# Streaming halves of weight blocks through six 2 KB places, keeping the other halves in pairs, and copying o1 in two parts

## The chip, the cores and the metric

The kernel runs as one program on one core of a Trainium2 chip. The metric is device time in microseconds (us) of one execution. Three runs of the kernel before took 2072.62, 2074.7 and 2076.44 us; the time that counts is their median, 2074.7 us.

## The reference, cut to what matters

Two independent heads share the output, and their results stand side by side in it. Head B is a long convolution over 2048 positions (by Fourier transforms) and does not change here. Head A is a recurrence over 64 segments of 32 rows, with a memory of 8 rows that each segment hands to the next:

```python
for s in range(n_seg):                                   # 64 segments
    xs = x[:, s * seg_len:(s + 1) * seg_len, :].copy()   # 32 rows
    h = jnp.concatenate([mem, xs], axis=1)               # 8 + 32 rows of 1024
    q = jnp.einsum('btd,dhe->bhte', h, Wq)               # 32 heads of 128
    k = jnp.einsum('btd,dhe->bhte', h, Wk)
    v = jnp.einsum('btd,dhe->bhte', h, Wv)
    scores = jnp.einsum('bhqe,bhke->bhqk', q, k) * scale
    scores = jnp.where(mask[None, None], scores, -1000000000.0)
    p = _softmax(scores, axis=-1)
    o = jnp.einsum('bhqk,bhke->bhqe', p, v)
    o = jnp.einsum('bhte,hed->btd', o, Wo)
    mem = o[:, :M, :].copy()                             # the next segment needs these 8 rows
    outs.append(o[:, M:, :])
```

So each segment multiplies by all of Wq, Wk, Wv and Wo, four bf16 matrices of 1024 x 4096 (8 MB each), and can begin only when the one before it has ended. The four matrices do not fit on the chip together with the rest.

## The kernel before, in words

**Stages.** Part B of the program (head B) fills the first 700 us. Beside it, work of head A that does not depend on the recurrence is done ahead: of every segment, 24 rows form, with the 8 memory rows, the 32 rows of the loop (the tile `hT`), and the keys, queries and values of the last 8 rows are computed before the loop and stored to DRAM (`PKd`, `VXd`). Then part A's loop over 64 segments runs (lines 357 to 583), and behind it one large product makes the output rows of those last 8 rows of all segments (lines 585 to 616).

**Weight blocks.** The weights are cut into 64 blocks of 128 rows by 2048 columns in bf16: 512 KB, or 4 KB in each of the 128 partitions. A block of k, q or v is named by matrix, column half t and row block kc; a block of o by u from 0 to 15, and holds two heads of 1024 columns each. A segment uses each block once, in one order: k of t = 0, q of t = 0, k and q of t = 1, v of t = 0, v of t = 1, then o 0 to 15.

**Where a block lies.** 49 blocks stay in SBUF (`RESIDENT`, loaded by `load_resident`, most of them during part B into places that part B has given up, the last 11 by `unit` in the first segment, where they are first used). Three blocks lie wholly or by half in PSUM (`KEPT`) and are copied out in each segment by VectorE (`fetch`, line 292). The other 12 (`STREAM`, `STREAM_O`) are loaded again in every segment: k 1 + 2, q 1 + 1, v 2 + 2, o 3. Before the loop they are copied to DRAM tiles of their own (`WD`, by `streamed_copies`, DRAM to DRAM during part B). In the loop `stage` (line 297) loads one whole block by one DMA of SyncE into the next of `SLOTS` = 4 places in turn (the tiles `wst`), so 16 KB of a partition serve as places. A load is issued as soon as the block that had the place, four loads earlier, has been used by TensorE. SyncE issues all of them in program order, and in the steady loop it issues nothing else; the loads of `PKd` and `VXd` and the two stores of a segment go out from ScalarE's DMA queue.

**The products.** In `quads` (line 365) a block of k, q or v takes 4 matmuls with 512 columns, one for each group of 32 columns of the array, side by side; in `oproj` (line 474) a block of o takes 8 with 256 columns. The weight columns are the moving operand. Four such matmuls together advance TensorE by about 0.21 us.

**The end of a segment.** `pv_x` makes the values of the second half of the heads in PSUM; `evac_o` (line 460) copies them to SBUF on ScalarE as `o1`, 128 x 512 in one instruction, while TensorE runs `oproj` for o 5, 6, 7 with `o0`. Then `oproj` for o 8 to 15 reads `o1`: an even u reads heads 0 and 1 of each group of four, an odd u heads 2 and 3. The output row block is copied (line 567), turned (line 573), and its memory rows enter `hT` (line 575) for the next segment. SBUF work tiles of the loop lie in one tile, `arena`.

In the traces an L365 or L474 matmul that reads `wst` reads a streamed block; one that reads `W`, `W_k`, `W_v`, `W_o`, `MF`, `Wlow` reads a resident one.

Of the kernel before, what the change touches and what calls it, by code (L numbers as in the profile page):

```python
# [10 lines left out]
BF16 = mybir.dt.bfloat16  # L11
# [10 lines left out]

STREAM = {("k", 0): (2,), ("q", 0): (2,), ("k", 1): (1, 5), ("q", 1): (4,), ("v", 0): (2, 7), ("v", 1): (4, 7)}
STREAM_O = (4, 8, 13)

BANK = {("k", 0): "b0", ("q", 0): "b1", ("k", 1): "b2", ("q", 1): "b0", ("v", 0): "b3", ("v", 1): "b2"}
KEPT = {("k", 0, 7): (("K7a", 0, 512), ("K7b", 512, 512), ("K7c", 1024, 512), ("K7d", 1536, 384), (None, 1920, 128)),
        ("q", 0, 7): (("Q7a", 1024, 512), ("Q7b", 1536, 512)),  # L30
        ("o", 15): (("Oa", 1024, 512), ("Ob", 1536, 384), (None, 1920, 128))}
HALF = (("q", 0, 7), ("o", 15))
SLOTS = 4

ARENA = 5984
AT = {"K7a": 3072, "K7b": 1024, "K7c": 2048, "K7d": 4192, "ob": 4960, "pk": 0, "vx": 3392, "Q7a": 2048, "Q7b": 3072,
# [18 lines left out]
    return src  # L55


def streamed_keys():
    return [key for key in [(m, t, kc) for (m, t), kcs in STREAM.items() for kc in kcs] + [("o", u) for u in STREAM_O]]


def streamed_copies(ctx, tc, src):
    nc = tc.nc
    dram = ctx.enter_context(tc.tile_pool(name="a_wd", bufs=1, space=bass.MemoryType.DRAM))
    out, copies = {}, []
    for key in streamed_keys():
        t_ = dram.tile([128, 2048], BF16, name="WD_%s" % "_".join(str(i) for i in key))
        copies.append(lambda t_=t_, key=key: nc.sync.dma_start(
            out=t_[:].rearrange("e (h d) -> e h d", h=2) if key[0] == "o" else t_[:], in_=src(key)))
        out[key] = t_  # L70
    return out, copies


class Ahead:
# [136 lines left out]
    return hT  # L211


RESIDENT = [(m, t, kc) for t in range(2) for m in "kq" for kc in range(8)] + [("v", t, kc) for t in range(2) for kc in range(8)] + [("o", u) for u in range(16)]
RESIDENT = [key for key in RESIDENT if key not in streamed_keys() and key not in KEPT]


class Keys(list):
    pass


EARLY = (3, 5)
LATE = 5


def load_resident(tc, pool, src, key, W_res, eng=None, t_=None):
    if t_ is None:
        t_ = pool.tile([128, 2048], BF16, name="W_%s" % "_".join(str(i) for i in key))
    (eng or tc.nc.sync).dma_start(out=t_[:].rearrange("e (h d) -> e h d", h=2) if key[0] == "o" else t_[:], in_=src(key))
    W_res[key] = t_  # L230


def part_a(ctx, tc, x, src, WD, HE, seg_len, out_a, ahead, W_res, rest, places, first):
    nc = tc.nc
    S, Dm = x.shape
    M = 8
    SL = seg_len
# [21 lines left out]
    between = {}  # L259

    def unit(key):
        if key in rest:

            rest.remove(key)
            load_resident(tc, wres, src, key, W_res, None, places.pop(0)() if places else None)
        if key in W_res:
            return W_res[key]
        if key in KEPT:
            return ahead_of.pop(key) + halves.get(key, [])
        between.pop(key, lambda: None)()  # L270
        if key in first:
            return first.pop(key)
        return stage(key, WD[key][:])

    ctx_l = ctx_w.enter_context(ExitStack())
    pers = ctx_l.enter_context(tc.tile_pool(name="a_pers", bufs=1))
# [14 lines left out]
    def words(out, in_):  # L291
        nc.vector.tensor_scalar(out=out.bitcast(I32), in0=in_.bitcast(I32), scalar1=0, scalar2=None, op0=ALU.bitwise_or)  # L292

    def stage(key, in_):
        t_ = wst.tile([128, 2048], BF16, name="wst", tag="w%d" % (loads[0] % SLOTS))
        loads[0] += 1
        nc.sync.dma_start(out=t_[:].rearrange("e (h d) -> e h d", h=2) if len(in_.shape) == 3 else t_[:], in_=in_)
        return t_

    def load_kept(key):  # L300
        t_ = first.pop(key) if key in first else stage(key, src(key))
        kept[key] = {}
        for n in (1,) if key in HALF else (0, 1):
            kept[key][n] = ps_k.tile([128, 512], F32, name="keep", tag="keep%d" % sum(len(b) for b in kept.values()))
            words(kept[key][n][:], t_[:, 1024 * n:1024 * n + 1024])
        if key in HALF:
            t_ = ahead.low["half"] if key[0] == "q" else wres.tile([128, 1024], BF16, name="Whalf")
            nc.sync.dma_start(out=t_[:], in_=src(key)[:, 0, :] if key[0] == "o" else src(key)[:, 0:1024])
            halves[key] = [(0, 1024, t_)]

    def fetch(key):
# [45 lines left out]
    for s in range(NS):  # L357
# [97 lines left out]
            pv(p[:], t, V, pb.rearrange("p a b c -> p a (b c)"), lbs)  # L455
            return p

        def evac_o(p, name):
            o = at(name, 4, 4, SL)
            nc.scalar.copy(out=o, in_=p[:].rearrange("p a (g q) -> p a g q", g=4))  # L460
            return o

        def pv_l(pl, t, V, L):
# [47 lines left out]
        nc.scalar.copy(out=QT1, in_=p1[:, 1])  # L511
        if s + 1 == NS:

            spare = [W_res[m, t, kc] for m, t in (("k", 0), ("q", 0), ("k", 1), ("q", 1), ("v", 0)) for kc in range(KC) if (m, t, kc) in W_res]
# [67 lines left out]
        if s + 1 < NS:  # L582
            stores(s, ob)

    order = sorted(range(16), key=lambda u: ("o", u) not in W_res)
    wo = {}
    for u in order:
        if ("o", u) in W_res:
            wo[u] = W_res["o", u]
        else:  # L590
            wo[u] = spare.pop(0)
            if ("o", u) in WD:
                nc.sync.dma_start(out=wo[u][:], in_=WD["o", u][:])
            else:
                nc.sync.dma_start(out=wo[u][:].rearrange("e (h d) -> e h d", h=2), in_=src(("o", u)))
    stores(NS - 1, ob)
    for j in range(2, 8):
        nc.sync.dma_start(out=raw[j][:], in_=OLd[j])
# [4 lines left out]
    for b in range(4):  # L603
        pe = [ps_k.tile([128, 512], F32, name="pe", tag="keep%d" % (2 * (b % 2) + n)) for n in range(2)]
        for u in order:
            for hh in range(2):
                h = 2 * u + hh
                hi = 16 * (h // 16) + 4 * (h % 4) + (h % 16) // 4
                for n in range(2):
                    nc.tensor.matmul(pe[n][:], lhsT=left[2 * b + hi // 16][:, 128 * (hi % 16):128 * (hi % 16) + 128],  # L610
                                     rhs=wo[u][:, 1024 * hh + 512 * n:1024 * hh + 512 * n + 512], start=(u == order[0] and hh == 0),
                                     stop=(u == order[-1] and hh == 1))
# [782 lines left out]
def kernel(  # L1395
# [33 lines left out]

    def residents(stay, early):  # L1430
        def put(t_):
            load_resident(tc, None, src, rest.pop(0), W_res, None, t_)
# [36 lines left out]

    low = low_blocks(ctx, tc)  # L1470
    ahead.low = low.pop()
    copies += [lambda t_=t_: load_resident(tc, None, src, rest.pop(0), W_res, None, t_) for t_ in low]

    def first_state(m0, xt):
        nc = tc.nc
# [49 lines left out]
```

## Time and profile before

| | us |
|---|---|
| three runs | 2072.62, 2074.7, 2076.44 (median 2074.7) |
| the profiled execution, its own time | 2080.33 |
| its span, first to last instruction | 2078.6 |
| part A's first segment (line 365's first matmul to the first transpose of line 573) | 705.45 to 753.47 |
| the next 62 segments, from transpose to transpose | 753.47 to 1996.36 |
| last segment and closing product | 1996.36 to 2078.6 |
| TensorE busy over the span | 1877.4 (90%) |
| weight loads of TensorE busy | 1188.3 (57%) |
| VectorE, ScalarE, GpSimd busy | 1415.5, 1047.8, 380.1 |
| mean granted TensorE clock | 0.975 |

The page gives busy shares for each engine and slices of the span in tenths; the queues' table gives the packets, bytes and the share of the core's 16 DMA engines that they took. "Idle before" a group of instructions is the idle time of its engine just before them, with what ended it. Matmuls overlap in the records, so a matmul's duration (382 ns) is longer than the time by which it moves TensorE on.

### The profile page before, as it was taken

What the parts mean: (1) busy time and instruction counts of PE and PEld (TensorE: products, weight loads), DVE (VectorE), ACT (ScalarE), POOL (GpSimd) and SP (SyncE); (2) the same over time, 40 slices, a digit from 0 to 9 for tenths busy, and PEclk for the clock granted to TensorE, in tenths of its full rate; (3) what the DMA queues carried; (4) which work ended last, traced back from release to release, by engine and by line L of the source; (5) the groups of instructions that cost most, each with busy time, mean ns of one, the idle gap of its engine ahead of it and who ended that gap; (6) DMA issues with size and microseconds to landing.
All of it is one profiled execution on the core that took longest, in us unless ns stands there. A gap on an engine that the chain in (4) does not pass through costs nothing. (4 is left out here: it accounts for less than half of the span.)

```text
span 2078.6 us, 78528 instructions
## 1 busy us (share of the span) xinstructions
PE 1877.4 (90%) x33734; PEld 1188.3 (57%) x33734; DVE 1415.5 (68%) x3352; ACT 1047.8 (50%) x1917; POOL 380.1 (18%) x748
## 2 busy tenths in 40 slices
PE   2799999977999779999999999999999999999999
PEld 1365666756888545555555555555555555555554
DVE  8689999989899346566666666656666666666650
ACT  5899999961333334444444444444444444444430
POOL 2133343452000011111111111111111111111120
PEclk8799999989999889999999999999999999999999
DMA  7697985665646999999999999999999999999991
GB/s 192 168 254 214 260 233 172 163 201 191 213 137 189 317 348 331 330 334 337 330 339 341 335 341 332 340 323 335 345 331 341 336 338 336 344 340 335 328 351 47
DMA packets 351187, 590.78 MB, mean 284 GB/s; under 512 B 108537, under 2 KB 228377, under 8 KB 348789
## 3 DMA queue, kind: packets, MB, share of 16 engines
q1 hardware_dynamic: 297016, 528.00, 75.4%
q10 hardware_dynamic: 44812, 28.26, 4.4%
q0 software_dynamic: 9008, 29.49, 4.3%
q8 instruction: 264, 4.33, 0.8%
q14 instruction: 87, 0.70, 0.1%
HBM read 530.86 MB, written 65.26 MB: 287 GB/s over the span
## 5 line engine op out<-in xcount | busy, mean ns | idle before, releaser
L365 PEld LDWEIGHTS <-a_hT 128*32 128x32 bf16 x12352 | 340.3, 96 | 294.1 <-issue 45.5
L371 ACT CAST arena<-acc 128x512 bf16<-128x512 f32 x384 | 225.1, 586 | 392.2 <-PE acc L365 333.6
L365 PE MATMUL acc<-W,a_hT 128*32 128x512 bf16 x4608 | 361.0, 382 | 0.6 <-issue 0.6
L474 PEld LDWEIGHTS <-arena 128*32 128x32 bf16 x8256 | 209.6, 96 | 110.2 <-ACT arena L460 54.7
L365 PE MATMUL acc<-wst,a_hT 128*32 128x512 bf16 x2304 | 231.9, 382 | 15.7 <-DMA wst<-WD_v 7.9
L292 DVE TENSOR_SCALAR arena<-keep 128x256 int32<-128x256 int32 (+1 forms) x512 | 176.2, 395 | 38.2 <-PE acc L365 35.1
L379 POOL COPY arena<-arena 128x128 bf16<-128x128 bf16 x128 | 37.6, 294 | 872.7 <-DMA arena<-PKd 311.4
L365 PE MATMUL acc<-MF,a_hT 128*32 128x512 bf16 x2048 | 172.5, 384 | 0.2 <-issue 0.2
L474 PE MATMUL pp<-W_o,arena 128*32 128x256 bf16 x4096 | 149.3, 275 | 5.4 <-DMA W_o<-in_A_Wo_dram 5.2
L167 PE MATMUL pro<-xTl,wsl 128*128 128x512 bf16 x512 | 123.0, 393 | 7.0 <-ACT xTl L111 4.9
L414 DVE TENSOR_REDUCE a_mx<-sc 128x4 f32<-128x160 f32 (+1 forms) x192 | 73.0, 380 | 82.4 <-ACT sc L410 82.4
L406 DVE TENSOR_REDUCE a_mx<-sc 128x4 f32<-128x160 f32 (+1 forms) x192 | 71.9, 374 | 79.5 <-PE sc L394 78.2
L1059 PEld LDWEIGHTS <-MF 128*128 128x128 bf16 x1024 | 103.1, 101 | 29.8 <-issue 8.6
L410 ACT ACTIVATE sc<-sc 128x160 f32<-128x160 f32 (+1 forms) x192 | 63.9, 333 | 108.0 <-DVE sc L407 85.1
L489 DVE COPY arena<-tr 128x512 bf16<-128x512 bf16 x64 | 27.2, 425 | 130.1 <-PE tr L376 130.1
L437 POOL TENSOR_TENSOR arena<-arena,a_BD 128x128 bf16<-128x128 bf16 x128 | 70.7, 552 | 227.7 <-DVE arena L424 204.6
L1059 PE MATMUL hps<-KT,MF 128*128 128x256 bf16 x720 | 94.7, 284 | 14.3 <-DVE x L1228 11.2
L567 ACT CAST arena<-pp 128x128 bf16<-128x128 f32 x128 | 27.7, 269 | 156.9 <-PE pp L474 156.9
L1286 PE MATMUL yp<-Bt,MI 128*128 128x256 bf16 x680 | 104.6, 274 | 0.8 <-ACT yb L1302 0.8
L1097 ACT ACTIVATE E<-pa 128x648 bf16<-128x648 f32 x128 | 91.4, 714 | 18.8 <-PE pa L1089 13.9
L460 ACT CAST arena<-pv 128x512 bf16<-128x512 f32 x128 | 75.3, 588 | 50.3 <-PE pp L444 39.7
L474 PE MATMUL pp<-wst,arena 128*32 128x256 bf16 x1536 | 77.2, 277 | 23.5 <-DMA wst<-WD_o 14.1
(313 smaller groups left out, 3976.0 us busy)
## 6 DMA issues: line engine op xcount, KB each, us to landing
wst<-WD_v SPq DMA_DIRECT2D x256, 512.0 KB
wst<-WD_k SPq DMA_DIRECT2D x192, 512.0 KB
wst<-WD_o SPq DMA_DIRECT2D x192, 512.0 KB
wst<-WD_q SPq DMA_DIRECT2D x128, 512.0 KB
Ud<-ux POOLq DMA_DIRECT2D x16, 1024.0 KB, 5.1
uq<-Ud SPq DMA_DIRECT2D x32, 512.0 KB
wsl<-in_A_Wk_dram SPq DMA_DIRECT2D x16, 512.0 KB
wsl<-in_A_Wv_dram SPq DMA_DIRECT2D x16, 512.0 KB
```

What stands on the lines that cost most here:

```text
L167: nc.tensor.matmul(a[:], lhsT=w[:, kc, 128 * j:128 * j + 128], rhs=xTl[:, kc, :, :].rearrange("p s k -> p (s k)"), start=(kc == 0), stop=( ...
L292: nc.vector.tensor_scalar(out=out.bitcast(I32), in0=in_.bitcast(I32), scalar1=0, scalar2=None, op0=ALU.bitwise_or)
L365: nc.tensor.matmul(a[32 * g:32 * g + 32, o_:o_ + rhs.shape[1]], lhsT=hT[:, kc, :], rhs=rhs, start=(kc == 0), stop=(kc == KC - 1), tile_pos ...
L371: nc.scalar.copy(out=q, in_=a[:])
L406: nc.vector.tensor_reduce(out=m_, in_=x, axis=AX.X, op=ALU.max)
L414: nc.vector.tensor_reduce(out=m_, in_=x, axis=AX.X, op=ALU.add)
L437: nc.gpsimd.tensor_tensor(out=L[:, 0].rearrange("p (a b) k -> p a b k", a=4), in0=bc(lt[:, :, 0:XL].unsqueeze(2), [128, 4, 4, XL]), in1=bc ...
L460: nc.scalar.copy(out=o, in_=p[:].rearrange("p a (g q) -> p a g q", g=4))
L474: nc.tensor.matmul(po[32 * qt:32 * qt + 32, o_:o_ + rhs.shape[1]], lhsT=oT[:, h % 4, (h % 16) // 4, :], rhs=rhs, start=False, stop=(h == 3 ...
L1059: pe.matmul(s_[r][half][:, cs, :], lhsT=MF[:, kc, 4 * rr + mc, cs, :], rhs=rhs, start=(i == 0 and mc == 0), stop=(i == 1 and mc == 3), ski ...
L1097: sc.activation(out=T["E", r, e // 4][:, lo:lo + 8 * NE].rearrange("p (i c) -> p i c", i=2), in_=T.pop(("p", r, e))[:, :, 0:4 * NE], func= ...
L1286: pe.matmul(yp[:, b, :], lhsT=m_[:, b, cs, kc, :], rhs=Bt[:, kc, j, half, c_, :], start=(kc == 0 and cs == 0 and half == 0), stop=(kc == 3 ...
```

## The change

`STREAM` now lists halves of blocks: 22 halves of 22 different blocks, each 128 x 1024 (256 KB, 2 KB in a partition). `SLOTS` is 6, and a place holds 2 KB, so 12 KB of a partition serve as places. The other halves of these 22 blocks stay in SBUF, two to one tile of 4 KB (`resident_items`), so there are 50 resident tiles, one more than before; one more is loaded early (`EARLY`). The DRAM tiles are 128 x 1024, and `streamed_copies` returns 11 functions that each issue two copies. `unit` returns both halves of a block as a list, which `columns` already accepts. `load_kept` stages halves, and of two of the kept blocks only the half that goes to PSUM. `o1` is copied in two instructions of 128 x 256, heads 0 and 1 of each group first, and `oproj` takes o 8, 10, 12, 14 before 9, 11, 13, 15. Behind the loop the closing product fills halves instead of whole blocks.

```diff
-STREAM = {("k", 0): (2,), ("q", 0): (2,), ("k", 1): (1, 5), ("q", 1): (4,), ("v", 0): (2, 7), ("v", 1): (4, 7)}
-STREAM_O = (4, 8, 13)
+STREAM = ((("k", 0, 2), 0), (("k", 0, 5), 1), (("q", 0, 2), 0), (("q", 0, 6), 1), (("k", 1, 2), 1), (("k", 1, 3), 0),
+          (("k", 1, 6), 0), (("q", 1, 1), 1), (("q", 1, 5), 1), (("v", 0, 1), 1), (("v", 0, 3), 1), (("v", 0, 7), 1),
+          (("v", 1, 2), 1), (("v", 1, 3), 1), (("v", 1, 4), 0), (("v", 1, 5), 1), (("o", 0), 0), (("o", 4), 1),
+          (("o", 6), 1), (("o", 10), 0), (("o", 11), 0), (("o", 13), 1))
...
-SLOTS = 4
+SLOTS = 6
...
+def part(src, key, h):
+    return src(key)[:, h, :] if key[0] == "o" else src(key)[:, 1024 * h:1024 * h + 1024]
...
+    for key, h in STREAM:
+        out[key, h] = dram.tile([128, 1024], BF16, name="WD_%s" % "_".join(str(i) for i in (*key, h)))
+
+    def copy(some):
+        for key, h in some:
+            nc.sync.dma_start(out=out[key, h][:], in_=part(src, key, h))
+    return out, [lambda i=i: copy(STREAM[i:i + 2]) for i in range(0, len(STREAM), 2)]
...
-EARLY = (3, 5)
+EARLY = (3, 6)
...
+        out = []
+        for h in range(2):
+            half = key, h
+            for item in [item for item in rest if half in item]:
+                rest.remove(item)
+                load_resident(tc, wres, src, item, W_res, places.pop(0)() if places and len(item) == 2 else None)
+            if half in W_res:
+                out.append((1024 * h, 1024, W_res[half]))
+            else:
+                out.append((1024 * h, 1024, first.pop(half) if half in first else stage(WD[half][:])))
+        return out
...
-    def stage(key, in_):
-        t_ = wst.tile([128, 2048], BF16, name="wst", tag="w%d" % (loads[0] % SLOTS))
+    def stage(in_):
+        t_ = wst.tile([128, 1024], BF16, name="wst", tag="w%d" % (loads[0] % SLOTS))
         loads[0] += 1
-        nc.sync.dma_start(out=t_[:].rearrange("e (h d) -> e h d", h=2) if len(in_.shape) == 3 else t_[:], in_=in_)
+        nc.sync.dma_start(out=t_[:], in_=in_)
         return t_
 
     def load_kept(key):
-        t_ = first.pop(key) if key in first else stage(key, src(key))
         kept[key] = {}
         for n in (1,) if key in HALF else (0, 1):
+            t_ = first.pop((key, n)) if (key, n) in first else stage(part(src, key, n))
...
-        def evac_o(p, name):
-            o = at(name, 4, 4, SL)
-            nc.scalar.copy(out=o, in_=p[:].rearrange("p a (g q) -> p a g q", g=4))
+        def evac_o(p, name, parts=1):
+            o, n = at(name, 4, 4, SL), 4 // parts
+            for i in range(0, 4, n):
+                nc.scalar.copy(out=o[:, i:i + n], in_=p[:, i:i + n, :].rearrange("p a (g q) -> p a g q", g=4))
             return o
...
-        o1 = evac_o(pv1, "o1")
+        o1 = evac_o(pv1, "o1", 2)
...
-        oproj(pp[:, 1, :], range(8, 16), o1)
+        oproj(pp[:, 1, :], (8, 10, 12, 14, 9, 11, 13, 15), o1)
...
-        for i, key in enumerate([("k", 0, 7)] + streamed_keys()[0:SLOTS - 1]):
-            first[key] = t_ = ahead.wst.tile([128, 2048], BF16, name="wst", tag="w%d" % i)
-            tc.nc.sync.dma_start(out=t_[:], in_=WD[key][:] if key in WD else src(key))
-            yield
+        for i, half in enumerate([(("k", 0, 7), 0), (("k", 0, 7), 1)] + list(STREAM[0:SLOTS - 2])):
+            first[half] = t_ = ahead.wst.tile([128, 1024], BF16, name="wst", tag="w%d" % i)
+            tc.nc.sync.dma_start(out=t_[:], in_=WD[half][:] if half in WD else part(src, *half))
+            if i % 2:
+                yield
```

More of the change, by code (lines that the diff above doesn't have):

```diff
@@ L55, in weight_blocks @@
     return src
-def streamed_keys():
-    return [key for key in [(m, t, kc) for (m, t), kcs in STREAM.items() for kc in kcs] + [("o", u) for u in STREAM_O]]
+def part(src, key, h):
+    return src(key)[:, h, :] if key[0] == "o" else src(key)[:, 1024 * h:1024 * h + 1024]
 def streamed_copies(ctx, tc, src):
@@ L64, in streamed_copies @@
     dram = ctx.enter_context(tc.tile_pool(name="a_wd", bufs=1, space=bass.MemoryType.DRAM))
[L65 to L71, printed above, removed]
+    out = {}
+    for key, h in STREAM:
[4 more added lines that the diff above has]
+    return out, [lambda i=i: copy(STREAM[i:i + 2]) for i in range(0, len(STREAM), 2)]
 class Ahead:
@@ L211, in constants, with resident_items, load_resident @@
     return hT
-RESIDENT = [(m, t, kc) for t in range(2) for m in "kq" for kc in range(8)] + [("v", t, kc) for t in range(2) for kc in range(8)] + [("o", u) for u in range(16)]
-RESIDENT = [key for key in RESIDENT if key not in streamed_keys() and key not in KEPT]
+EVERY = [(m, t, kc) for t in range(2) for m in "kq" for kc in range(8)] + [("v", t, kc) for t in range(2) for kc in range(8)] + [("o", u) for u in range(16)]
+def resident_items():
+    out, open_ = [], None
+    for key in EVERY:
+        halves = [(key, h) for h in range(2) if (key, h) not in STREAM]
+        if key in KEPT or not halves:
+            continue
+        if len(halves) == 2:
+            out.append(tuple(halves))
+        elif open_ is None:
+            open_ = len(out)
+            out.append(tuple(halves))
+        else:
+            out[open_] += tuple(halves)
+            open_ = None
+    if open_ is not None:
+        out.append(out.pop(open_))
+    return out
+RESIDENT = resident_items()
 class Keys(list):
     pass
-EARLY = (3, 5)
+EARLY = (3, 6)
 LATE = 5
-def load_resident(tc, pool, src, key, W_res, eng=None, t_=None):
+def load_resident(tc, pool, src, item, W_res, t_=None):
     if t_ is None:
-        t_ = pool.tile([128, 2048], BF16, name="W_%s" % "_".join(str(i) for i in key))
-    (eng or tc.nc.sync).dma_start(out=t_[:].rearrange("e (h d) -> e h d", h=2) if key[0] == "o" else t_[:], in_=src(key))
-    W_res[key] = t_
+        t_ = pool.tile([128, 1024 * len(item)], BF16, name="W_%s" % "_".join(str(i) for i in item[0][0]))
+    if len(item) == 2 and item[0][0] == item[1][0]:
+        key = item[0][0]
+        tc.nc.sync.dma_start(out=t_[:].rearrange("e (h d) -> e h d", h=2) if key[0] == "o" else t_[:], in_=src(key))
+    else:
+        for n, (key, h) in enumerate(item):
+            tc.nc.sync.dma_start(out=t_[:, 1024 * n:1024 * n + 1024], in_=part(src, key, h))
+    for n, half in enumerate(item):
+        W_res[half] = t_[:, 1024 * n:1024 * n + 1024]
+    W_res[item] = t_
 def part_a(ctx, tc, x, src, WD, HE, seg_len, out_a, ahead, W_res, rest, places, first):
@@ L261, in unit @@
     def unit(key):
[L262 to L267, printed above, removed]
+        between.pop(key, lambda: None)()
         if key in KEPT:
             return ahead_of.pop(key) + halves.get(key, [])
[L270 to L273, printed above, removed]
+        out = []
[6 more added lines that the diff above has]
+                out.append((1024 * h, 1024, W_res[half]))
+            else:
+                out.append((1024 * h, 1024, first.pop(half) if half in first else stage(WD[half][:])))
+        return out
     ctx_l = ctx_w.enter_context(ExitStack())
@@ L292, in words @@
         nc.vector.tensor_scalar(out=out.bitcast(I32), in0=in_.bitcast(I32), scalar1=0, scalar2=None, op0=ALU.bitwise_or)
-    def stage(key, in_):
-        t_ = wst.tile([128, 2048], BF16, name="wst", tag="w%d" % (loads[0] % SLOTS))
+    def stage(in_):
+        t_ = wst.tile([128, 1024], BF16, name="wst", tag="w%d" % (loads[0] % SLOTS))
         loads[0] += 1
-        nc.sync.dma_start(out=t_[:].rearrange("e (h d) -> e h d", h=2) if len(in_.shape) == 3 else t_[:], in_=in_)
+        nc.sync.dma_start(out=t_[:], in_=in_)
         return t_
     def load_kept(key):
-        t_ = first.pop(key) if key in first else stage(key, src(key))
         kept[key] = {}
         for n in (1,) if key in HALF else (0, 1):
+            t_ = first.pop((key, n)) if (key, n) in first else stage(part(src, key, n))
             kept[key][n] = ps_k.tile([128, 512], F32, name="keep", tag="keep%d" % sum(len(b) for b in kept.values()))
-            words(kept[key][n][:], t_[:, 1024 * n:1024 * n + 1024])
+            words(kept[key][n][:], t_[:])
         if key in HALF:
             t_ = ahead.low["half"] if key[0] == "q" else wres.tile([128, 1024], BF16, name="Whalf")
-            nc.sync.dma_start(out=t_[:], in_=src(key)[:, 0, :] if key[0] == "o" else src(key)[:, 0:1024])
+            nc.sync.dma_start(out=t_[:], in_=part(src, key, 0))
             halves[key] = [(0, 1024, t_)]
@@ L512, in part_a @@
         if s + 1 == NS:
-            spare = [W_res[m, t, kc] for m, t in (("k", 0), ("q", 0), ("k", 1), ("q", 1), ("v", 0)) for kc in range(KC) if (m, t, kc) in W_res]
+            spare = [t_ for m, t in (("k", 0), ("q", 0), ("k", 1), ("q", 1), ("v", 0), ("v", 1)) for item, t_ in W_res.items()
+                     if len(item) == 2 and item[1] not in (0, 1) and item[0][0] == item[1][0] and item[0][0][0:2] == (m, t)]
+            assert sum(item[0][0][0:2] != ("v", 1) for item in RESIDENT if len(item) == 2 and item[0][0] == item[1][0] and item[0][0][0] != "o") >= 16
             raw, left = ([spare.pop(0) for _ in range(8)] for _ in range(2))
@@ L583, in part_a @@
             stores(s, ob)
-    order = sorted(range(16), key=lambda u: ("o", u) not in W_res)
-    wo = {}
+    order = sorted(range(16), key=lambda u: sum((("o", u), h) not in W_res for h in range(2)))
+    wo, over = {}, []
     for u in order:
[L588 to L595, printed above, removed]
+        for h in range(2):
+            half = ("o", u), h
+            if half in W_res:
+                wo[half] = W_res[half]
+                continue
+            if not over:
+                t_ = spare.pop(0)
+                over += [t_[:, 0:1024], t_[:, 1024:2048]]
+            wo[half] = over.pop(0)
+            nc.sync.dma_start(out=wo[half], in_=WD[half][:] if half in WD else part(src, *half))
     stores(NS - 1, ob)
@@ L610, in part_a @@
                     nc.tensor.matmul(pe[n][:], lhsT=left[2 * b + hi // 16][:, 128 * (hi % 16):128 * (hi % 16) + 128],
-                                     rhs=wo[u][:, 1024 * hh + 512 * n:1024 * hh + 512 * n + 512], start=(u == order[0] and hh == 0),
+                                     rhs=wo[("o", u), hh][:, 512 * n:512 * n + 512], start=(u == order[0] and hh == 0),
                                      stop=(u == order[-1] and hh == 1))
@@ L1431, in put @@
         def put(t_):
-            load_resident(tc, None, src, rest.pop(0), W_res, None, t_)
+            load_resident(tc, None, src, rest.pop(0), W_res, t_)
         for _ in range(EARLY[0]):
@@ L1471 @@
     ahead.low = low.pop()
-    copies += [lambda t_=t_: load_resident(tc, None, src, rest.pop(0), W_res, None, t_) for t_ in low]
+    copies += [lambda t_=t_: load_resident(tc, None, src, rest.pop(0), W_res, t_) for t_ in low]
     def first_state(m0, xt):
```

## The prediction

> **What bounds the kernel now.** I read the page first, for where the time lies.
>
> ```profile
> PE   2799999977999779999999999999999999999999
> ...
> DMA  7697985665646999999999999999999999999991
> ```
>
> From slice 14 on (728 us) both rows stand at 9, and they stay there through the loop, 64% of the span. Next, busy time by stage:
>
> ```profile
> core 0: us, PE busy (x) PEld busy (x) DVE busy (x) ACT busy (x) POOL busy (x), PEclk, DMA share, GB/s
> ...
> 700.00:750.00 50.00, 31.27 (x424) 15.97 (x425) 17.26 (x48) 11.64 (x22) 3.04 (x7) 0.72 0.97 346
> ...
> 1000.00:1200.00 200.00, 189.50 (x4254) 110.50 (x4250) 125.45 (x390) 89.24 (x200) 28.87 (x70) 1.00 0.95 336
> ```
>
> In the loop TensorE is busy for 94.8% and the DMA engines for 95%; VectorE has 63%. The 62 segments between 753.47 and 1996.36 take 20.05 us on average, the shortest 19.13, the longest 22.28. So two resources are close to full. The waits of PE between 800 and 2000 us tell which one costs time:
>
> ```profile
> PE pp L474 <- DMA wst<-WD_o: 11.9, 17, 1.5
> PE pp L474 <- ACT arena L460: 6.7, 32, 0.3
> PE acc L365 <- DMA wst<-WD_k: 6.1, 12, 1.1
> PE acc L365 <- DMA wst<-WD_v: 5.4, 12, 0.9
> PE sc L390 <- POOL arena L379: 4.6, 15, 0.9
> ```
>
> Over the whole loop (from the timeline) waits for streamed blocks are 27.4 us, waits for the POOL copy of `PKd` 5.3, for the copy of `o1` 7.6, and for no releaser that the profile shows ("issue") 7.4. The POOL copy itself waits for a DMA: the load of `PKd` lands 4.6 to 7.6 us after its issue. The chain that ended last shows the same loads:
>
> ```profile
> 1636.52 6.89 DMA arena<-PKd
> ...
> 1669.86 5.77 DMA wst<-WD_o
> ```
>
> Now the DMA work of a segment, from the queues between 1000 and 1800 us:
>
> ```profile
> q1 hardware_dynamic: 69136, 251.75, 88.0%
> q10 hardware_dynamic: 22630, 15.12, 6.2%
> ```
>
> q1 holds SyncE's loads: 88.0% of 20.05 is 17.64 us of all 16 engines for 12 blocks, 1.47 us each. Everything else is 7.4%, 1.48 us. Together 19.1 us, as much as the shortest segment: a hiccup can't be caught up, and that is why single blocks come late in every second segment or so.
>
> **The change, part by part.**
>
> *Bytes.* 22 halves are 11 blocks: one block of 12 is no longer loaded. At the rate of the row above a half takes 0.735 us, 22 take 16.2, with the rest 17.65 us per segment against 19.1. What rows of 2 KB cost in the loop isn't in the trace. The nearest row is the first segment, where blocks of Wo come straight from the input in 2 KB rows, between 734 and 752 us:
>
> ```profile
> DMA packets 3089, 7.10 MB, mean 394 GB/s; under 512 B 212, under 2 KB 212, under 8 KB 3086
> ...
> q1 hardware_dynamic: 3086, 7.07, 103.6%
> ```
>
> 2,874 packets of 2 KB and more carry 7.07 MB: two thirds of the bytes go in 2 KB packets. They take 2.64 us of the 16 engines per MB; the loop's 4 KB packets take 2.80. That end gives 16.7 us per segment. The other end is a lone store of 256 KB in 2 KB rows at the end (`out_dram<-W`), 1.0 us of the 16 engines with its start and end: 22 x 1.0 + 1.48 = 23.5 us. I take 0.735, since the first row has queue, direction and full rings in common with the loop. Break-even with today's 19.1 is 0.80 us per half, 9% more.
>
> The Trainium skill, page "DMA: Bandwidth & Descriptors", speaks against halves: "Rules for kernel authors" asks for 1 MiB or more per DMA, and "Anatomy of one DMA" gives, for GpSimd's path, 2.0 us plus bytes over 436 GB/s. An estimate by that, one after the other: 22 x 2.6 = 57 us for halves, 12 x 3.2 = 38 us for blocks, so 19 us more per segment. The row of 12 blocks in 20.05 us shows that the fixed part overlaps while several are queued.
>
> *Issues.* SyncE issues 22 instead of 12, 0.32 us each (the tile's rows): 7.0 of 19 us; nothing else is in its queue in the loop, so this is covered.
>
> *Places.* Six halves instead of four blocks are on the way: 4.4 us of transfer instead of 5.9. A load is issued when its place is free. The tightest case after is v 1 5, which takes the place of v 0 1: from the segment at 1016 us, v 0 1 ends about 1025.0 and v 1 5 starts 1029.70, less a stall of 1.09 in between: 3.6 us. Before, the tightest is o 13 after v 1 4: 1029.7 to 1035.2, 5.45 us. A half needs, with an empty queue, about 1.2 us to its first bytes (that store: issued 2074.6, moving from 2075.8), 0.73 to move and 0.7 until it is seen (the last load of `OLd`: bytes to 2031.1, VectorE starts 2031.85): 2.65 us. About 0.9 us is left there, against 2 before. So the DMA has 1.3 us per segment to spare where it had none, but less reserve at v 1 3 to v 1 5, four streamed blocks in a row.
>
> Of the 32.7 us of waits for `wst` and `PKd` I therefore take two thirds off: 22 us. Bounds: all of it (33), or 0 if the shorter reserve eats it; beyond 0 is a rival.
>
> *o1 in two parts.* In one segment PE shows:
>
> ```profile
> 1012.09 0.84 PE L474 MATMUL pp<-W_o,arena 128*32 128x256 bf16 x24
> 1013.14 0.40 PE L474 MATMUL pp<-wst,arena 128*32 128x256 bf16 x8 [0.21 <-ACT arena L460]
> ```
>
> Three blocks of o should take 0.65 us; the next starts after 1.05. In 55 of 61 segments it starts within 0.08 us of the end of ScalarE's copy, and the median loss is 0.39 us, so the copy is on the path in nearly every segment. The copy of 512 columns takes 588 ns (L460), one of 128 columns 269 (L567); on the line between, 256 columns take 375. `oproj` can start 0.21 us earlier: 63 x 0.21 = 13 us. The second part ends at most 0.75 us after the start of the first, and four blocks of o (0.86 us) run before it is needed. Behind it on ScalarE is only the copy of L567, which waits 2.75 us for PE anyway. Bounds: 0 (a late block of o hides it) to 20.
>
> *Before and after the loop.* The kept q 7 and o 15 are staged by half, and one more resident block comes in early: one 512 KB load less in the DMA-bound first segment, where blocks follow at 1.35 us: -1.4 (bounds -3 and +2, as SyncE reaches the last Wo loads behind other places). Part B's extra issues are hidden: DMA share 0.55 to 0.88 there, TensorE or VectorE at 92% and more; without that cover 11 x 0.5 us. The closing product runs 55 us without a wait, and its first need of a late tile (2032.2) lies 6 us behind the last copy it needs.
>
> *Sum.* 22 + 13 + 1.4 = 36 us off the profiled execution's 2080.3 (span 2078.6): 2044. That run is 0.27% above the median of 2074.7; the same difference from the median gives 2038. The segment would be 19.5 us. By the bounds together: 33 + 20 + 3 off gives 2019, and 0 gives 2075.
>
> **The rivals.**
>
> *Only o1 counts.* Waits for halves take the place of waits for blocks, because the reserve shrinks as much as the load. For it: the 0.9 us of reserve. Against it: 1.3 us of spare DMA time. 5 to 14 us off: 2061 to 2070. If the gain of o1 is also swallowed, no change within 4 us (0.2%, about what a measurement of this kernel can tell).
>
> *Slower: the landing of a half is a latency, not a queue.* Now a load takes 5.8 us from issue to use when it is late (chain), and `PKd`, only 128 KB, at least 4.6. I ascribe most of it to up to three blocks ahead in the rings. If a half still takes 5 us with a shorter queue, v 1 5 is 1.4 us late in each segment, and that is more than the 0.6 gained: about +0.8 x 63 = 50 us, 2125. It decides from a landing time of 3.6 + 0.6 us on.
>
> *Slower: 2 KB rows.* From 0.80 us per half the DMA is the bound; each further percent is 0.18 us per segment, 11 us in all. At 0.85: +1.1 us, 2144. The first segment's packets speak against it, though TensorE ran there at half clock and drew less from SBUF.
>
> That the change would not cut the bytes can be excluded: 22 x 256 KB against 12 x 512 KB is in the lists.
>
> **How the numbers follow.** Forecast (15 to 65 us off) 0.70; only o1 0.10; no change 0.03; short reserve 0.12; 2 KB rows 0.05. So faster 0.80, same 0.03, slower 0.17. The range reaches from 2010 (the bounds, and waits without releaser that shrink with them) to 2084, which leaves out about 0.17: most of the slower cases and little else. The forecast's own range is 2010 to 2060.
>
> **What would show it.** Segments of 19.3 to 19.7 us; DMA share 0.90 to 0.95 with q1 at 0.73 to 0.76 us per half; the wait for L460 gone; waits for `wst` under 15 us, the rest at v 1 4, v 1 5 and o 13; the POOL copy's wait for `PKd` shorter. Wrong if waits for `wst` at v 1 3 to v 1 5 exceed 0.5 us per segment, or if q1 takes more than 0.80 us per half.

## The result and the profile after

The changed kernel takes 2099.99 us (median of 4 runs, 2090.8 to 2112.88) against 2075.57 for the kernel before (4 runs): a ratio of 1.0126, interval 1.0094 to 1.0158. It is slower by 24 us, above the upper end of the range. The profiled execution is the longest of the four: 2112.88 us, span 2111.2.

The difference lies in the loop. The first transpose comes at 753.25 us (753.47 before), so the time ahead of the loop is unchanged. The 62 segments behind it end at 2025.98 (1996.36): 20.53 us each instead of 20.05, the shortest 19.42 instead of 19.13. (The profiled run lies 12.9 us above its median, the one of before 5.6: 0.2 and 0.1 us of a segment. Between the medians a segment lost some 0.4 us, not 0.48.) On the page of the changed kernel, busy tenths in 40 slices:

```profile
PE   2699999878899789999999999999999999999989
DMA  7697985755646999999999899998999989999991
```

The row of the DMA engines, which stood at 9 through the loop, now has slices of 8. The same in numbers, busy time by stage:

```profile
core 0: us, PE busy (x) PEld busy (x) DVE busy (x) ACT busy (x) POOL busy (x), PEclk, DMA share, GB/s
1000.00:1200.00 200.00, 191.08 (x4181) 110.44 (x4173) 122.55 (x383) 88.51 (x207) 28.93 (x70) 1.00 0.92 305
```

The rate fell from 336 to 305 GB/s and the share from 0.95 to 0.92: fewer bytes were asked for, and the time grew all the same. TensorE does fewer matmuls in these 200 us (4181 records against 4254) and still shows more busy time, which is explained below. The waits of PE from 800 to 2000 us:

```profile
PE acc L399 <- DMA wst<-WD_v: 29.4, 64, 2.1
PE acc L399 <- DMA wst<-WD_k: 7.1, 15, 1.2
PE pp L509 <- DMA wst<-WD_o: 3.5, 10, 0.9
```

L399 is the old L365, L509 the old L474. Waits for v rose from 5.4 to 29.4 us, those for o fell from 11.9 to 3.5. The wait for ScalarE's copy of `o1` (6.7), the one for GpSimd's copy of `PKd` (4.6 before, 0.2 now) and those without a releaser are as good as gone. Streamed blocks together (those for q with them, 1.0 and 0.7): 41 us, against 24 in the same window before.

That is 17 us more, and the waits that went away come to about as much. By this table nothing should have been lost, but the segments lost 30 us. The loss is seen in the mean lengths of the stretches of a segment, between markers on TensorE's timeline:

| stretch | before, us | after, us |
|---|---|---|
| k of t = 0, q of t = 0, k 1 0 to 2 | 4.89 | 4.86 |
| k 1 3 to 5 | 1.49 | 1.30 |
| k 1 6 and 7, q of t = 1, v 0 0 to 2 | 3.23 | 3.36 |
| v 0 3 to 7 | 1.85 | 1.90 |
| v 1 0 to 5 | 1.83 | 2.84 |
| v 1 6 and 7, o 0 to 4 | 2.65 | 2.61 |
| o 5 to 15 | 3.61 | 3.18 |
| output, transpose, memory rows | 0.48 | 0.49 |

One stretch, the one with four streamed halves in a row, lost 1.01 us of its own; the end of o gained 0.43; the others moved little. What happens there is seen in the segment at 1070 us. SyncE issues the halves of v 1 2, 3, 4 and 5 (timeline: start, length, engine):

```profile
1070.22 0.32 SPq L331 DMA_DIRECT2D wst<-WD_v  x1
1070.88 0.32 SPq L331 DMA_DIRECT2D wst<-WD_v  x1
1071.74 0.32 SPq L331 DMA_DIRECT2D wst<-WD_v  x1
1072.61 1.44 SPq L331 DMA_DIRECT2D wst<-WD_v  x1
```

TensorE's matmuls on them, from its timeline (in brackets the recorded wait):

```profile
1075.33 0.39 PE L399 MATMUL acc<-wst,a_hT 128*32 128x512 bf16 x2
1075.43 0.40 PE L399 MATMUL acc<-W,a_hT 128*32 128x512 bf16 x2
1076.00 0.39 PE L399 MATMUL acc<-wst,a_hT 128*32 128x512 bf16 x2 [0.17 <-DMA wst<-WD_v]
1076.67 0.39 PE L399 MATMUL acc<-wst,a_hT 128*32 128x512 bf16 x2 [0.28 <-DMA wst<-WD_v]
...
1077.34 0.39 PE L399 MATMUL acc<-wst,a_hT 128*32 128x512 bf16 x2
```

The four halves are used at 1075.33, 1076.00, 1076.67 and 1077.34: 0.67 us apart instead of the 0.21 that a block takes, and each 4.7 to 5.1 us after its own issue. The trace marks the completion of each of the 16 pieces in which a load comes; the last marks of these four stand at 1075.29, 1075.96, 1076.63 and 1077.30, 0.04 us ahead of each use, so TensorE started as soon as a half was there. (The last of the four issues took 1.44 us, the longest at v 1 5 in the loop, where the mean is 0.47. Why isn't known.) Only 0.45 us of the lost time stands there as a wait. A block is now two resident and two streamed matmuls, and the resident pair's modelled end covers the gap: this is the nearest reading of the surplus of busy time, and of why the table of waits shows less than was lost. The chain of waits puts the last of the four as one piece (start, length):

```profile
1072.61 4.69 DMA wst<-WD_v
```

### The profile page after: what moved, and what is told of

Same layout as the page of the kernel before. It is cut to its first block, busy times and chain, and to the rows that moved or that the text cites. A ratio compares the mean times of both kernels' runs of the same rounds, so it can differ in the third digit from the quotient of the medians.

```text
span 2111.2 us, 79896 instructions
## 1 busy us (share of the span) xinstructions
PE 1907.7 (90%) x33734; PEld 1196.1 (57%) x33734; DVE 1417.1 (67%) x3352; ACT 1054.0 (50%) x1981; POOL 385.4 (18%) x748
## 4 chain that ended last, share of the span: by engine, by line
PE 54%; DMA 26%; ACT 11%; DVE 5%; SPq 2%; issue 2%; ACTq 0%; POOL 0%; DVEq 0%; POOLq 0%
PE acc L399 22%; DMA wst<-WD_v 13%; PE pp L509 10%; DMA wst<-WD_k 5%; PE hps L1098 4%; PE yp L1325 4%; DMA wst<-WD_o 3%; PE pe L649 3%; ACT sn L1153 2%; ACT E L1136 2%; ACT nr L1162 2%; PE pv L478 2%; PE pro L170 1%; DMA out_dram<-uu 1%; PE pa L1128 1%
## 5 line engine op out<-in xcount | busy, mean ns | idle before, releaser
L399 PEld LDWEIGHTS <-a_hT 128*32 128x32 bf16 x12352 | 344.2, 96 | 378.0 <-issue 134.6
L399 PE MATMUL acc<-wst,a_hT 128*32 128x512 bf16 x2048 | 391.8, 383 | 49.1 <-DMA wst<-WD_v 36.2
L399 PE MATMUL acc<-W,a_hT 128*32 128x512 bf16 x4608 | 413.3, 382 | 0.0
L509 PEld LDWEIGHTS <-arena 128*32 128x32 bf16 x8256 | 214.9, 97 | 79.3 <-issue 38.3
L399 PE MATMUL acc<-MF,a_hT 128*32 128x512 bf16 x2048 | 171.2, 381 | 0.0
L509 PE MATMUL pp<-W_o,arena 128*32 128x256 bf16 x4096 | 148.4, 275 | 4.6 <-DMA W_o<-in_A_Wo_dram 4.5
L495 ACT CAST arena<-pv 128x256 bf16<-128x256 f32 (+1 forms) x192 | 79.0, 445 | 146.9 <-PE pp L478 104.5
L399 PE MATMUL acc<-W_v,a_hT 128*32 128x512 bf16 x1536 | 122.9, 384 | 0.0
L509 PE MATMUL pp<-wst,arena 128*32 128x256 bf16 x1536 | 110.6, 277 | 7.7 <-DMA wst<-WD_o 5.7
L471 POOL TENSOR_TENSOR arena<-arena,a_BD 128x128 bf16<-128x128 bf16 x128 | 66.0, 515 | 173.7 <-DVE arena L458 139.0
```

Source lines behind the costliest of these rows:

```text
L399: nc.tensor.matmul(a[32 * g:32 * g + 32, o_:o_ + rhs.shape[1]], lhsT=hT[:, kc, :], rhs=rhs, start=(kc == 0), stop=(kc == KC - 1), tile_pos ...
L471: nc.gpsimd.tensor_tensor(out=L[:, 0].rearrange("p (a b) k -> p a b k", a=4), in0=bc(lt[:, :, 0:XL].unsqueeze(2), [128, 4, 4, XL]), in1=bc ...
L495: nc.scalar.copy(out=o[:, i:i + n], in_=p[:, i:i + n, :].rearrange("p a (g q) -> p a g q", g=4))
L509: nc.tensor.matmul(po[32 * qt:32 * qt + 32, o_:o_ + rhs.shape[1]], lhsT=oT[:, h % 4, (h % 16) // 4, :], rhs=rhs, start=False, stop=(h == 3 ...
```

## The experiments

All ratios are to the kernel before, run in the same turn on the same chip. "Segment" is the mean of the 62 segments in the profiled run.

**e1: only o1 in two parts**, in the kernel before.

```
-        o1 = evac_o(pv1, "o1")
+        o1 = evac_o(pv1, "o1", 2)
...
-        oproj(pp[:, 1, :], range(8, 16), o1)
+        oproj(pp[:, 1, :], (8, 10, 12, 14, 9, 11, 13, 15), o1)
```

> The kernel before with only the o1 edit: two copies of 128 x 256 and o 8, 10, 12, 14 ahead of 9, 11, 13, 15. The changed kernel's stretch from the second pv to pl is 0.43 us per segment shorter than before (3.18 against 3.61). Theory A (the o1 copy was on the path, and its gain stands by itself): that stretch falls to 3.2 to 3.3 us and 63 x 0.2 to 0.4 = 13 to 27 us come off, 2048 to 2062. Rival (the DMA engines are the bound in the loop, a faster end of the segment only makes the next streamed block late): the stretch gets shorter, waits for wst grow by as much, total within 4 us of before.

Measured: 0.9985 [0.9963, 1.0006], 10 runs; segment 19.99, the stretch of o 5 to 15 3.45 instead of 3.61. The wait for the copy fell from 6.7 to 0.6 us in the profile, but the time hardly moved. The nearest reading is that the loop gets its blocks from the DMA no sooner.

**e4: the changed kernel without that edit** (evacuation and order of o as before).

> The changed kernel with o1 copied in one instruction again and o 8 to 15 in their old order. Theory A: the stretch from the second pv to pl goes back from 3.18 to 3.4 to 3.6 us, but part of it is won back as the halves of v 1 come less late: 2105 to 2127. If the v 1 halves alone set the pace (a segment lasts as long as its 22 loads): within 5 us of the changed kernel's 2100.

Measured: 1.0196 [1.0159, 1.0233]; segment 20.49. Against 1.0126 with the edit, it is worth about 0.7%, 14 us, in the changed kernel by the medians; the two intervals just touch, and the segments of the two profiled runs (20.49 and 20.53) don't show it. The profile of the changed kernel shows no gap at the first block that reads `o1`, o 8: the 16 matmuls of o 7 and o 8 take 0.44 us from the first line to the second, as long as two blocks take.

```profile
1061.01 0.61 PE L509 MATMUL pp<-W_o,arena 128*32 128x256 bf16 x16
1061.45 0.28 PE L509 MATMUL pp<-wst,arena 128*32 128x256 bf16 x4
```

So o1 is not what made it slower.

**e2 and e5: the cost of 2 KB rows, and of twice as many DMAs**, both in the kernel before with its 12 blocks and four places. Both keep a block in DRAM as two halves of 128 rows of 2 KB. e2 loads a block by two DMAs, e5 by one (the lines of the load alone):

```
+            for h in range(2):                                                          # e2
+                nc.sync.dma_start(out=t_[:, 1024 * h:1024 * h + 1024], in_=WD[key][h])
+            nc.sync.dma_start(out=t_[:].rearrange("e (h d) -> e h d", h=2),             # e5
+                              in_=WD[key][:].rearrange("h e d -> e h d"))
```

> The kernel before with the same 12 whole blocks in the same four 4 KB places, but each block loaded as two DMAs of 256 KB with rows of 2 KB, from DRAM tiles that hold the halves one behind the other. Places, bytes, list and time of release stay as before; only the row and the number of DMAs change. Theory A (only the reserve and the list of streamed halves made the change slower): within 8 us of before, q1 stays at 1.47 us of the 16 engines per block. Theory B (short rows or more DMAs cost DMA time, 0.79 us per half as in the changed kernel's q1 row): 24 x 0.79 + 1.5 = 20.5 us per segment, the DMA is the bound, segments of 20.7 to 21.3 us, 2115 to 2155.

> The kernel before with 12 whole blocks in four 4 KB places and one DMA of 512 KB per block, whose rows are 2 KB (256 packets; the DRAM tile holds the halves one behind the other). With two DMAs of 256 KB in the same places the run took 16 us more than before, and q1 took 2.90 us of the 16 engines per MB against 2.80. Theory A (the row length is what costs: in the packet records a 2 KB packet takes 84 ns in the median, a 4 KB packet 159, so two short ones 6% more): as that run, 2.88 to 2.95 us per MB, 8 to 20 us above before. Rival (the number of DMAs costs, each with its own start and its 16 completions): as before, within 4 us of it, 2.80 us per MB.

Measured: e2 1.0080 [1.0052, 1.0108], e5 0.9983 [0.9959, 1.0007]. The queue of SyncE's loads from 1000 to 1800 us (packets, MB, share of the 16 engines), e2 first:

```profile
q1 hardware_dynamic: 137500, 250.37, 90.8%
```

```profile
q1 hardware_dynamic: 131421, 253.36, 90.9%
```

Rows of 2 KB raise the busy time from 2.80 to 2.87 us per MB and cost no time. Splitting a block over two DMAs costs about 1%, 16 to 20 us, for 12 DMAs more per segment, with the same bytes and rows and the same 16 KB. The changed kernel has 10 more than before. The Trainium skill, page "DMA: Bandwidth & Descriptors", section "Rules for kernel authors", asks for 1 MiB or more per DMA; two DMAs of 256 KB against one of 512 KB agree with its direction. An estimate from the fixed 2.0 us that the same page's "Anatomy of one DMA" gives for GpSimd's path, 12 more of them one after the other, is 24 us per segment. Measured, e2's segment is 0.28 us longer than e5's.

**e3: the four streamed halves of v 1 spread apart** (v 1 0, 2, 4, 7 instead of 2, 3, 4, 5).

> The changed kernel with one edit: of v of t = 1 the blocks 0, 2, 4, 7 are streamed by half instead of 2, 3, 4, 5. Bytes, rows, places and number of DMAs stay. Theory A (four streamed halves in a row ask for loads faster than they land, 0.67 us apart): the stretch from the scores of t = 1 to the first pv, 2.84 us against 1.65 in a segment without a wait, falls to 1.7 to 2.3, 0.4 to 0.9 us come off in each segment, 2045 to 2075. Theory B (the DMA engines are simply full because 2 KB rows cost more): the waits only move to other blocks, 2090 to 2105.

Measured: 1.0148 [1.0105, 1.0191], no better than the changed kernel. The stretch v 1 0 to 5 fell from 2.84 to 2.33 us, and the next two rose by 0.20 and 0.18. Waits for o rose to 18.7 us from 3.5. The loss was moved on: it doesn't belong to those four halves alone.

**e8: all 22 halves spread evenly**, six places.

> The changed kernel with the same 22 halves and six places, but the streamed blocks spread evenly over the time of a segment, one about every 0.86 us. Theory A (a round of a place, from one issue to the next into the same place, cannot be shorter than 5.5 to 5.9 us with 12 KB of places, as in all runs that had 12 KB: 6 x 20.53 / 22 = 5.60 for the changed kernel, 3 x 22.95 / 12 = 5.74, 3 x 21.65 / 11 = 5.90): 22 x 5.55 / 6 = 20.3 us per segment whatever the list, 2085 to 2105. Rival (the four streamed blocks in a row are the reason): segments of 19.3 to 19.7 us, 2030 to 2060.

Measured: 1.0047 [1.0031, 1.0062]; segment 20.08. The list is worth about 0.8%, 16 us, but with this list too the kernel doesn't reach the time before.

**e6 and e10: whole blocks in 12 KB.** e6 is the kernel before with three places for its 12 blocks. e10 has also 11 blocks instead of 12, 50 resident, and o1 in two parts: all that the change does, with whole blocks.

```
-SLOTS = 4
+SLOTS = 3                  # e6 and e10
-STREAM_O = (4, 8, 13)
+STREAM_O = (4, 13)         # e10 alone
```

> The kernel before with three 4 KB places instead of four; the same 12 whole blocks, 4 KB rows. 12 KB on the way instead of 16, as in the changed kernel. Theory A (the shorter reserve costs time by itself): more waits for wst, segments of 20.5 to 21.5 us, 2100 to 2165. Rival (the DMA engines are the bound whatever lies ahead, places only hold what has landed early): within 8 us of before.

> The changed kernel's memory and bytes without halves: three 4 KB places, 50 resident blocks, 11 whole blocks streamed (o 8 is resident), 4 KB rows, o1 in two parts. Theory A (12 KB of places is the reason that the change is slower): no faster than the changed kernel, 2090 to 2125. Theory B (2 KB rows are the reason): the 8% fewer bytes count, q1 2.80 us per MB, segments of 19.2 to 19.7 us, 2025 to 2055.

Measured: e6 1.0926 [1.0879, 1.0973], e10 1.0517 [1.046, 1.0575]. One place less of four costs 9% with no other edit, and nearly all waits of PE are then for `wst` (800 to 2000 us, e6):

```profile
PE pp L474 <- DMA wst<-WD_o: 60.3, 75, 2.4
PE acc L365 <- DMA wst<-WD_v: 47.0, 74, 1.9
PE acc L365 <- DMA wst<-WD_k: 43.3, 68, 1.6
```

The share of the DMA engines fell to 0.87 meanwhile: they idle while TensorE waits for them. In the same 12 KB, the halves of the change are far better than whole blocks (1.0126 against 1.0517).

**e9 and e11: halves, but more of them, so that more places fit.** 24 evenly spread halves through eight places (49 resident, as before), and 23 through seven.

> The changed kernel with 24 halves, spread evenly over the time of a segment, through eight 2 KB places (16 KB, as before the change) and 49 resident tiles. Bytes as before the change, rows 2 KB, o1 in two parts. Theory A (the reserve and the list are what made it slower): waits for wst under 0.4 us per segment, 2050 to 2075. Theory B (the rows): 6% more DMA time than before at the same bytes, 2085 to 2110.

> The changed kernel with 23 halves, evenly spread, through seven 2 KB places (14 KB); one half tile is resident alone. Same memory. Theory A (rounds of 5.5 to 5.9 us): 23 x 5.6 / 7 = 18.4 us, so the places no longer set the pace; a segment then lasts as with eight places and 24 halves (19.89 us) or a little less for the 4% fewer bytes, 19.5 to 19.9 us, 2045 to 2072. Rival (the bytes or the number of DMAs set the pace, places don't): between the 22 halves and the 24, 2070 to 2095.

Measured: e9 0.9984 [0.9957, 1.0012], e11 0.9989 [0.9969, 1.0009], segments 19.89 and 19.78. With 14 KB of places or more the loss is gone, but the bytes are then 23 and 24 halves, and in e9 q1's share is 91.3%, which with the 7.5% of the rest is 98.8% of the 16 engines.

**e12: five places instead of six**, the changed kernel otherwise.

> The changed kernel with five 2 KB places instead of six, all else alike. Theory A (the round of a place sets the pace): 22 x 5.5 / 5 = 24.2 us per segment, 63 x 3.7 = 230 us more than the changed kernel, 2300 to 2350. Rival (the DMA engines' work sets the pace): within 20 us of the changed kernel's 2100.

Measured: 1.0649 [1.063, 1.0669], segment 22.01. The direction is as expected, the size is not: I had taken the time from one load into a place to the next for a fixed round of about 5.5 us, and it went down to 5 x 22.01 / 22 = 5.0.

**e13, e14, e15: eight places, without loading more.** These kernels leave out the weights of one block: v 1 7 (in e15 v 1 6) is multiplied from another block's tile, which frees 4 KB. TensorE does the same work, but the output is not the reference's. e13 is the changed kernel with its own list, e14 has the even list, e15 whole blocks (11 of them, as in e10) in four places.

```
-SLOTS = 6
+SLOTS = 8
+SHARED = {("v", 1, 7): ("v", 1, 6)}     # e14: ("v", 1, 4); e15: SLOTS = 4, ("v", 1, 6): ("v", 1, 5)
...
+        key = SHARED.get(key, key)
```

> The changed kernel with eight 2 KB places instead of six and nothing else: the same 22 halves, 2 KB rows, o1 in two parts. The 4 KB come from a block left out: v 7 of t = 1 is multiplied from the resident tile of v 6 of t = 1, so the numbers of that block are not the reference's, while TensorE does the same work and the DMA loads one resident block less before the loop. Theory A (the places, 12 KB instead of 16, are what the change lost by; its bytes and its o1 are a gain): waits at v 1 2 to 5 under 0.2 us, segments of 19.2 to 19.5 us, 2025 to 2045, 55 to 75 under the changed kernel. Rival (the number of 256 KB DMAs, or the DMA engines' work, is the bound): 2070 to 2100, segments of 19.8 us and more.

> The even list of 22 halves with eight places, 4 KB freed in the same way (v 7 of t = 1 is multiplied from the tile of v 4). Theory A: with 16 KB of places the list matters little, within 8 us of the changed kernel's list with eight places, 2020 to 2045. Rival (list and places each take their part): 15 us and more under it.

> 11 whole blocks through four 4 KB places, o1 in two parts, 4 KB freed in the same way (v 6 of t = 1 is multiplied from the tile of v 5); against three places, which took 2182, only the fourth place and one resident tile differ. Theory A: 2020 to 2045, as 22 halves with eight places. Rival (two 256 KB DMAs cost more than one of 512 KB, as the run with two DMAs per block showed by 16 us): 10 to 20 us under 22 halves with eight places.

Measured: e13 2034.69 us, 0.9781 [0.9749, 0.9812]; e14 0.9734 [0.9703, 0.9765]; e15 0.9817 [0.9786, 0.9848]. Two places more turn +1.3% into -2.2%; nothing else in the loop differs, and ahead of it one resident block less is loaded (first transpose at 751.07 us instead of 753.25). e13's waits of PE, and its busy time by stage, in the windows used above (L401 and L511 there are L399 and L509):

```profile
PE acc L401 <- DMA wst<-WD_v: 4.5, 11, 0.7
PE acc L401 <- issue: 1.5, 2, 1.3
PE pp L511 <- DMA wst<-WD_o: 1.0, 1, 1.0
```

```profile
1000.00:1200.00 200.00, 196.85 (x4415) 114.42 (x4415) 129.48 (x408) 92.12 (x219) 30.04 (x73) 1.00 0.97 324
```

Waits for streamed blocks are 5.5 us instead of 41; the stretch v 1 0 to 5 takes 1.88 us instead of 2.84; TensorE has 98% and 4415 matmuls in the 200 us.

All of these on one scale. The round is the mean time from one load into a place to the next one into it: segment x places / loads. It has to hold the landing, the wait for TensorE's turn and the use. The landing is the mean time from a load's issue to the last of its 16 completion marks, over the 62 segments. Late are the loads of a segment on which TensorE starts within 0.12 us of that mark.

| kernel | loads | places | KB | segment, us | round, us | landing, us | late | ratio |
|---|---|---|---|---|---|---|---|---|
| e12 | 22 halves | 5 | 10 | 22.01 | 5.0 | 4.08 | 7.4 | 1.065 |
| e8, even | 22 halves | 6 | 12 | 20.08 | 5.5 | 4.46 | 3.9 | 1.005 |
| after | 22 halves | 6 | 12 | 20.53 | 5.6 | 4.39 | 4.7 | 1.013 |
| e6 | 12 blocks | 3 | 12 | 22.95 | 5.7 | 5.10 | 7.5 | 1.093 |
| e10 | 11 blocks | 3 | 12 | 21.65 | 5.9 | 5.01 | 5.6 | 1.052 |
| e11, even | 23 halves | 7 | 14 | 19.78 | 6.0 | 4.76 | 3.7 | 0.999 |
| e9, even | 24 halves | 8 | 16 | 19.89 | 6.6 | 5.12 | 3.8 | 0.998 |
| before | 12 blocks | 4 | 16 | 20.05 | 6.7 | 5.66 | 2.0 | 1 |
| e14, even | 22 halves | 8 | 16 | 19.22 | 7.0 | 4.73 | 0.2 | 0.973 |
| e13 | 22 halves | 8 | 16 | 19.40 | 7.1 | 4.67 | 0.8 | 0.978 |
| e15 | 11 blocks | 4 | 16 | 19.59 | 7.1 | 5.55 | 1.3 | 0.982 |

With the same loads, fewer places make the segment longer each time: 22 halves with 8, 6 and 5 places, 12 and 11 blocks with 4 and 3. The landing hardly moves with it (4.67, 4.39 and 4.08 us for the halves), so it is not the load that gets slower but the time left for it that shrinks. The round is worked out from the segment itself, so it sums this up and proves nothing of its own. No version that makes the whole product beat the kernel before by more than the measurement tells: 22 halves with eight places lack 4 KB of SBUF.

## Why the prediction was wrong, point by point

**The step that failed: places.** The prediction set 3.6 us from free place to use at v 1 5 against 2.65 us that a half needs, and concluded that 0.9 us was left. The 2.65 did not hold. It was put together from an empty queue (a lone store, the last load). In the changed kernel's loop a half lands 4.39 us after its issue on average, at v 1 5 4.48 us (3.47 to 5.96 over the 62 segments), and TensorE starts within 0.12 us of the landing at v 1 4 in 60 of the 62 segments and at v 1 5 in all. Against 3.6 that is 0.9 us late, where the stretch lost 1.01 us on average. The kernel before had the right number on its own page: late blocks stood in the chain with 5.8 us, against a shortest reserve of 5.45. The change takes 1.85 us from the reserve and 1.27 us from the landing (5.66 to 4.39).

**So the rival came true**: the landing outlasts the reserve, and 4.48 us lies above the 4.2 (3.6 + 0.6) from which on it was to decide. With 4.48 in place of its 5 us the rival's own sum gives 0.28 us in each of 63 segments, 18 us, 2092; 2100 was measured, and its own 50 us (2125) were twice too many. Its "a latency, not a queue" holds in the main. A half lands after 4.08 us with three earlier loads still on their way at its issue, after 4.43 with four, after 4.46 with five, where a queue alone would add the 0.67 us that the halves stand apart in the segment shown for each. The sign named for "wrong", waits at v 1 3 to v 1 5 over 0.5 us per segment, is missed in the table of waits (0.46) and met by the starts: the start of v 1 5 lies 1.80 us behind that of v 1 2 on average, and 0.85 in e13.

e13 shows that this is the cause, and not only one that fits. It gives v 1 5 the place of q 1 1 instead of v 0 1. The half lands no sooner there, 4.89 us after its issue, but TensorE's start on it lies 5.2 us after the issue on average, where the shortest in the changed kernel is 3.52, and the loss is gone. e3 and e8 show that it isn't those four halves alone: in all three lists tried with 12 KB about four loads or more in a segment are late.

**Two thirds of the waits off, 22 us.** Same step, other end. Waits for `wst` in the window went from 24 to 41 us instead of under 15. e13, with 5.5, shows that bytes saved do take the waits away, if the reserve is kept.

**Bytes.** 0.735 us per half was forecast; 84.5% of the 800 us at q1 over 855 halves is 0.79, outside the 0.73 to 0.76 given. In e13 it is 0.77 and in e14 as well. The rows of 2 KB are 2.5% of that (e5). Still 22 x 0.79 and the rest of 1.56 are 18.9 us, under the shortest segment, so the DMA's rate isn't what set the time: it was mis-sized without deciding. (The 1.3 us to spare of the prediction are 19.1 less 17.65, 1.45, by its own terms.) The rival of the 2 KB rows falls by e5. A busy share is no price, either: the busy time per MB rises where less is in flight (2.80 us before with four blocks, 2.95 in e6 with three, by 80.9% of 800 us over 219.26 MB).

**Issues.** Covered on SyncE, as said: SyncE waits for places most of the time. But "covered there" was taken for "free", and e2 prices twelve more DMAs in the loop of the kernel before at some 16 us. Where the reserve is long this price isn't seen: 22 halves (e13) take no longer than 11 blocks (e15).

**o1.** 13 us forecast; 14 by the medians in the changed kernel (e4), and not told from nothing alone (e1, 4 us by the medians). The size may be right, but the bound of 0 is what e1 shows. Of the 0.43 us that the stretch of o 5 to 15 gained, e1's edit alone gives 0.16, and the halves without it (e4, 3.32) give 0.29. In e13, which has both, the stretch is 3.40 long again. So a part of the 3.18 is likely work that other engines caught up with while TensorE waited at v 1: in e13's segment at 1018 us ScalarE's copy of `o1` starts behind its softmax instruction (1018.84, the copy 1019.04), and in the changed kernel's at 1060 that instruction is over by 1060.11 and the copy waits for TensorE until 1060.72. No run tests this.

**Start.** -1.4 us forecast; -0.2 seen at the first transpose. Nothing hangs on it, nor on the first reading of the page: TensorE's row still stands at 7 in the slice from 728 us on and at 9 from 780.

**The sum.** e13 is 45 us under the kernel before of its own turn, where 36 were forecast, with a segment of 19.40 where it was 19.5. So the forecast fits a kernel that gives up no places, though not term by term (o1's part is unsure). One latency, taken from an empty queue, changed its sign.

**What stays open.** Why a half in the loop lands only after 4.4 us, where the prediction's pieces from an empty queue make 2.65; the packet records show a candidate for the segment shown (last section), but no run tried it. Nor was it settled what holds e9 and e11 at 19.8 to 19.9 us: they have 23 and 21 us of waits for `wst` between 800 and 2000 us, about as many as the kernel before (24), and full engines are the nearest reading for e9.

## What to carry to other kernels

When a stream of loads runs through places, compare each load's time from free place to use with the time from issue to landing that the same stream shows when it is busy, not with one load in an empty queue. The chain of waits of the kernel before names it where a load is late, and the completion marks give it for every load. Memory taken from the places to keep more blocks resident gives up time to cover the landing for fewer bytes: here 4 KB of places were worth 3.4% of the time, more than the 2.2% that the rest of the change brings when they stay. Smaller pieces make more of the same places (halves against blocks: 4% in 12 KB, and 0.4%, inside the intervals, in 16 KB), and an even spread brought 0.5 to 0.8%.

## What the runs showed that I had not expected

- Whether a load is late shows little in the rate. With three places for whole blocks (e6) the DMA engines are busy for 87% of the time and TensorE waits 161 us for them.
- Each load has 16 completion marks, and a matmul that waits for it starts 0.04 us after the last. The marks of one load come in over 1.75 us on average in the changed kernel (2.06 before), though a packet of 2 KB takes 84 ns (4 KB: 159 ns). So it is the slowest of the 16 pieces that sets the landing.
- Among the same packets are 16 KB ones of the instruction queue, one every 6.2 us or so, some 1.05 us each. In the segment shown, one of 1.69 us began at 1072.10; the first piece of v 1 2 was in at 1072.97 and the last at 1075.29, and the next three halves were complete 0.67 us after each other, as long as eight packets of 84 ns take, a sixteenth of a half. It looks as if one late piece after another had set all four. That such a packet holds up a piece, and with it a block, is a reading of these records alone.
- TensorE's busy time rises when it waits between the matmuls of one block: 191.08 us with 4181 matmuls in the changed kernel, 189.50 with 4254 before. For such a block the distance between starts shows the loss, not the table of waits.
